# Neighborhood attention on one core: values projected for two strips at once, emptied over all 128 partitions, with a transfer of one half

## The chip, the core and the metric

One core of a Trainium2 chip runs the kernel. The metric is the device time in microseconds (us) of one execution; a time quoted for a kernel is the median of its runs, each beside runs of the kernel before on the same chip.

In the profile PE is the matmul engine, PEld its weight load, DVE the vector engine, ACT the scalar engine, POOL the engine called GpSimd, and SP the engine that only issues transfers here.

## The reference, cut to what matters

```python
x: [1, 224, 224, 192] bf16      wqkv: [192, 576]      wo: [192, 192]
ks, dil = 7, 2                                  # a 7 x 7 neighborhood, every second row and column
q, k, v = split(x @ wqkv)
...                                             # indices of the 49 neighbors of each pixel, clipped at the edges
logits = einsum('bnc,bnkc->bnk', q, k[neighbors]) * 192 ** -0.5
p = softmax(logits)
out = einsum('bnk,bnkc->bnc', p, v[neighbors]) @ wo
```

## The kernel before

The picture has 14 strips of 16 rows. Dilation 2 splits rows and columns into even and odd: `rc` is the row parity and `cc` the column parity. A **step** (rc, j) makes 8 rows of one parity around the border between strips j-1 and j. There are 28 steps, in the order (0,0), (1,1), (0,1), (1,2), (0,2), (1,3) and so on. A step has 7 **ticks**. In each tick PE makes 16 score matmuls (`s_stage`), ACT takes exp of them, PE makes 8 value matmuls into the one `y` bank (`v_stage`), and DVE takes reciprocal and product out of that bank (`out_stage`). The remaining slot of a tick goes to a **filler**: value projections for the next step (`v_unit`), or one of four query and edge items.

The weights are folded, so the "keys" are x itself, only rearranged. A strip is read by one transposing load into `xt`; POOL then copies it, parity by parity, into `XA` and `XB`; and both the scores and the value projections read those copies.

```python
def load_xt(b):                                  # one strip, 4 buffers, all on SP's queue
    t = xt_pool.tile([128, 3, 16, S], BF, name=f"xt{b}", tag="xt")
    nc.sync.dma_start_transpose(out=..., in_=xp[16 * (b % NJ): ...])

def make_keys(k, rc):                            # four copies on POOL
    for cc in range(2):
        for kt in range(2):
            key_copy(k, rc, cc, kt, nc.gpsimd.tensor_copy)

def half(k, cc):
    return 64 * ((k + cc) % 2)                   # which 64 partitions strip k has in VW

def v_unit(k, rc, n0, n1):                       # one strip, 4 tiles of columns: 16 matmuls
    def emit():
        pv = ps_go.tile([128, 2, 2, 256], F32, name="pv", tag="go")
        for n in range(n0, n1):
            for kt in range(2):
                for cc in range(2):
                    h = half(k, cc)
                    nc.tensor.matmul(pv[h:h + 64, ..., 0:C], lhsT=keys(k, rc, cc, kt)[:, n, :],
                                     rhs=WP[:, cc, kt, :], start=(kt == 0), stop=(kt == 1))
        for cc, eng in ((0, nc.vector.tensor_copy), (1, nc.scalar.copy)):
            hs = slice(half(k, cc), half(k, cc) + 64)
            eng(out=VW[hs, rc, cc, n0:n1, 0:C], in_=pv[hs]...)        # 64 partitions x 768
        ...                                       # the two are declared independent
    return emit

# the loop over the steps, cut to the parts in question
    if rc == 1 or si == 0:
        load_xt(j + 2)                           # at the start of step (1, j)
    for ti, i in enumerate(range(NQ - 1, -1, -1)):
        T = s_stage(rc, j, i)
        if pend:
            v_stage(pend)
            out_stage(pend)
        ...                                      # fillers: projections, query items
        if ti == 2 and si + 2 < len(steps) and si > 0:
            make_keys(steps[si + 2][1], steps[si + 2][0])
```

The softmax here doesn't subtract the row's maximum and nothing guards it: scores larger than these inputs give would overflow.

## Time and profile before

The time before was 352.73 us (median of 3 runs, 351.33 to 355.38).

| what | busy us | share of the span |
|---|---|---|
| PE | 317.1 | 90% |
| DVE | 261.8 | 74% |
| ACT | 254.1 | 72% |
| POOL | 248.6 | 71% |

The page of the kernel before: busy times, the TensorE clock over 40 slices of the span (9 is 90% or more), the transfers, the chain of work that ended last by engine, and the groups (busy us, mean ns of one, then idle time just before it and what ended most of that).

```profile
PE 317.1 (90%) x7686; PEld 290.5 (83%) x7686; DVE 261.8 (74%) x554; ACT 254.1 (72%) x414; POOL 248.6 (71%) x525
...
PEclk9998999999999999999999999999999999999995
...
DMA packets 112369, 43.81 MB, mean 125 GB/s; under 512 B 86900, under 2 KB 111838, under 8 KB 112290
...
PE 56%; DVE 29%; issue 7%; POOL 2%; ACT 2%; DMA 1%; POOLq 0%; DVEq 0%
...
L482 DVE TENSOR_TENSOR o_sb<-y,rs 128x384 bf16<-128x384 f32 x162 | 101.1, 624 | 6.2 <-DVE rs L477 0.6
L286 ACT CAST vw<-pv 64x768 bf16<-64x768 f32 (+2 forms) x116 | 82.7, 713 | 31.5 <-PE pv L281 21.0
L286 DVE CAST vw<-pv 64x768 bf16<-64x768 f32 (+2 forms) x116 | 98.7, 851 | 2.2 <-PE pv L281 0.3
```

Two readings matter. First, PE is busy nine tenths of the time and is most of the chain; DVE is the next in it. Second, the evictions of the projections (`vw<-pv`) cost DVE 98.7 us and ACT 82.7 us, and each uses only 64 of the 128 partitions.

PE's waits in the kernel before (us in total, times, longest):

```profile
PE y L432 <- DVE o_sb L482: 11.9, 52, 0.9
PE y L432 <- ACT p_sb L419: 2.9, 2, 2.6
```

And the timeline of DVE in the middle of the run (start, length), which shows where the first of them comes from:

```profile
168.31 0.56 DVE L482 TENSOR_TENSOR o_sb<-y,rs 128x384 bf16<-128x384 f32 x1
168.90 0.96 DVE L286 CAST vw<-pv 64x768 bf16<-64x768 f32 x1
169.90 0.17 DVE L477 RECIPROCAL rs<-y 128x2 f32<-128x2 f32 x1
170.10 0.56 DVE L482 TENSOR_TENSOR o_sb<-y,rs 128x384 bf16<-128x384 f32 x1
```

DVE works in order. An eviction of 0.96 us sits between two turns of the `y` bank, and the value matmuls of the next tick can't start before the product at 170.10 has ended.

### The profile page before, as it was taken

How to read it: one execution, taken by the hardware profiler on the slowest of the kernel's cores; microseconds unless marked ns; L12 is line 12 of the kernel's file. 1: busy time of each engine (PE TensorE's matmuls, PEld its weight loads, DVE VectorE, ACT ScalarE, POOL GpSimd, SP SyncE). 2: the span in 40 equal slices, each digit the busy share in tenths (PEclk: the TensorE clock that was granted, in tenths of full speed). 3: DMA queues.
4: the chain of work that ended last, by engine and by line, in shares of the span. 5: the costliest groups of instructions: out<-in, count | busy, mean ns of one | idle time of the engine just before them, and what ended most of it. 6: DMA issues, size and time to landing. Idle time of an engine off the chain costs nothing.

```text
span 351.5 us, 17929 instructions
## 1 busy us (share of the span) xinstructions
PE 317.1 (90%) x7686; PEld 290.5 (83%) x7686; DVE 261.8 (74%) x554; ACT 254.1 (72%) x414; POOL 248.6 (71%) x525
## 2 busy tenths in 40 slices
PE   8969899999999899998999999999899999999850
PEld 5549789988899789998889998899888999988740
DVE  8687897777777687786787777877677787768750
ACT  3437888877788688787877878778777688768730
POOL 7497988676786669666776678666785678757670
PEclk9998999999999999999999999999999999999995
DMA  8975583864928728365293472834928539222112
GB/s 190 198 172 137 131 193 105 149 157 93 185 80 123 161 62 202 83 152 133 63 188 98 103 185 60 195 91 98 188 72 135 150 73 208 72 67 68 40 43 81
DMA packets 112369, 43.81 MB, mean 125 GB/s; under 512 B 86900, under 2 KB 111838, under 8 KB 112290
## 3 DMA queue, kind: packets, MB, share of 16 engines
q1 hardware_dynamic: 109490, 41.06, 52.3%
q0 software_dynamic: 2432, 1.39, 1.6%
q8 instruction: 60, 0.98, 1.2%
q10 hardware_dynamic: 368, 0.22, 0.2%
q14 instruction: 19, 0.16, 0.2%
HBM read 0.29 MB, written 19.35 MB: 56 GB/s over the span
## 4 chain that ended last, share of the span: by engine, by line
PE 56%; DVE 29%; issue 7%; POOL 2%; ACT 2%; DMA 1%; POOLq 0%; DVEq 0%
PE y L432 19%; DVE o_sb L482 15%; PE pg L357 12%; PE pv L281 8%; DVE vw L286 7%; PE s_88 L416 5%; DVE rs L477 5%; PE pe L313 4%; PE s_87 L416 4%; PE y L185 1%; POOL out_dram L449 1%; DVE oall L482 1%; DMA out_dram<-o_sb 1%; ACT vw L286 1%; DVE xa_90 L256 1%
## 5 line engine op out<-in xcount | busy, mean ns | idle before, releaser
L432 PE MATMUL y<-vw,p_sb 128*48 128x193 bf16 (+1 forms) x1540 | 104.3, 249 | 19.0 <-DVE o_sb L482 11.9
L482 DVE TENSOR_TENSOR o_sb<-y,rs 128x384 bf16<-128x384 f32 x162 | 101.1, 624 | 6.2 <-DVE rs L477 0.6
L286 ACT CAST vw<-pv 64x768 bf16<-64x768 f32 (+2 forms) x116 | 82.7, 713 | 31.5 <-PE pv L281 21.0
L286 DVE CAST vw<-pv 64x768 bf16<-64x768 f32 (+2 forms) x116 | 98.7, 851 | 2.2 <-PE pv L281 0.3
L432 PEld LDWEIGHTS <-p_sb 128*48 128x48 bf16 (+1 forms) x1540 | 75.9, 106 | 28.6 <-issue 22.5
L477 DVE RECIPROCAL rs<-y 128x2 f32<-128x2 f32 x168 | 28.5, 170 | 63.0 <-PE y L432 61.7
L419 ACT ACTIVATE p_sb<-s_88 128x448 bf16<-128x448 f32 x98 | 53.5, 546 | 14.2 <-PE s_88 L416 13.7
L447 POOL DMA_DIRECT2D out_dram<-o_sb x27 | 15.6, 577 | 63.8 <-DVE o_sb L482 63.8
L419 ACT ACTIVATE p_sb<-s_87 128x448 bf16<-128x448 f32 x98 | 53.4, 545 | 4.3 <-PE s_87 L416 3.6
L357 PEld LDWEIGHTS <-aw 128*64 128x64 bf16 x1008 | 52.1, 112 | 4.4 <-DVE vw L286 1.4
L416 PEld LDWEIGHTS <-xa_91 128*64 128x64 bf16 x532 | 50.6, 111 | 1.1
L416 PEld LDWEIGHTS <-xa_90 128*64 128x64 bf16 x532 | 49.4, 111 | 2.4 <-DVE ga_98 L361 1.1
L416 PEld LDWEIGHTS <-xa_92 128*64 128x64 bf16 x476 | 45.5, 111 | 1.2
L416 PEld LDWEIGHTS <-xb_94 128*64 128x64 bf16 x420 | 38.3, 111 | 2.0 <-issue 1.3
L416 PEld LDWEIGHTS <-xb_93 128*64 128x64 bf16 x420 | 36.3, 111 | 0.9
L361 ACT CAST hs<-pg 128x848 bf16<-128x848 f32 x27 | 23.4, 865 | 16.4 <-PE pg L357 7.9
L416 PEld LDWEIGHTS <-xb_95 128*64 128x64 bf16 x364 | 32.2, 111 | 1.0
L416 PEld LDWEIGHTS <-xb_96 128*64 128x64 bf16 x336 | 30.2, 111 | 0.6
L281 PE MATMUL pv<-WP,xa_90 128*64 128x192 bf16 x280 | 28.2, 248 | 0.3 <-DVE vw L286 0.3
L281 PE MATMUL pv<-WP,xa_91 128*64 128x192 bf16 x280 | 27.7, 246 | 0.2 <-DVE vw L286 0.2
L361 ACT CAST ga_98<-pg 128x848 bf16<-128x848 f32 x27 | 23.4, 865 | 5.1 <-PE pg L357 4.0
L361 ACT CAST ga_99<-pg 128x848 bf16<-128x848 f32 x26 | 22.5, 865 | 4.2 <-PE pg L357 3.0
(231 smaller groups left out, 1038.2 us busy)
## 6 DMA issues: line engine op xcount, KB each, us to landing
out_dram<-o_sb SPq DMA_DIRECT2D x162, 96.0 KB
out_dram<-o_sb SPq DMA_DIRECT2D x27, 60.0 KB
out_dram<-oe POOLq DMA_DIRECT2D x27, 18.0 KB, 3.1
out_dram<-o_sb POOLq DMA_DIRECT2D x27, 18.0 KB, 2.7
xb_95<-xb_93 SPq DMA_DIRECT2D x4, 112.0 KB
xb_96<-xb_94 SPq DMA_DIRECT2D x4, 112.0 KB
out_dram<-oall SPq DMA_DIRECT2D x8, 36.0 KB
out_dram<-oall POOLq DMA_DIRECT2D x8, 36.0 KB, 2.1
```

The lines of the kernel that those rows point to most:

```text
L185: nc.tensor.matmul(y_bank[:, 1, 1, 0:128], lhsT=ident[:], rhs=ident[:], start=True, stop=True, skip_group_check=True)
L281: nc.tensor.matmul(pv[h:h + 64, (n - n0) // 2, (n - n0) % 2, 0:C], lhsT=keys(k, rc, cc, kt)[:, n, :], rhs=WP[:, cc, kt, :], start=(kt == 0 ...
L286: ins.append(eng(out=VW[hs, rc, cc, n0:n1, 0:C], in_=pv[hs].rearrange("p a b c -> p (a b) c")[:, 0:n1 - n0, 0:C]))
L313: nc.tensor.matmul(pg[64 * h:64 * h + 64, g, par::2, :], lhsT=AW[w][:, 64 * h:64 * h + 64], rhs=r, start=(i == 0), stop=(i == 1))
L357: nc.tensor.matmul(pr[64 * h:64 * h + 64, g, a_ - 4 * g:b_ - 4 * g, :], lhsT=AW[w][:, 64 * h:64 * h + 64], rhs=xt[b][:, k, l, :], start=(i ...
L361: return eng(out=dst[:, 6:S].rearrange("p s (g r) -> p s g r", r=4), in_=pr[ps, :, :, 3:S - 3].rearrange("p g r s -> p s g r"))
L416: nc.tensor.matmul(o[h:h + 64, :, rs], lhsT=keys(k, rc, cc, kt)[:, n, :], rhs=(A, Bt)[kt][:, cc, CW * n:CW * n + QW, rs], start=(kt == 0), ...
L419: nc.scalar.activation(out=T.p[:].rearrange("p a b -> p (a b)"), in_=ps[:, 0:4 * QW * BR], func=ACTF.Exp)
L432: nc.tensor.matmul(o, lhsT=l, rhs=rhs, start=st, stop=True, skip_group_check=True)
L447: q.dma_start(out=dst, in_=src[8 * s0:8 * s1])
L477: nc.vector.reciprocal(out=rs[:], in_=y_bank[:, sls, :, C:C + 1])
L482: nc.vector.tensor_tensor(out=o[:], in0=y_bank[:, sls, :, 0:C], in1=rs[:].to_broadcast([128, nt, 2, C]), op=ALU.mult)
```

## The change: its intent, and the diff

The intent is to make each eviction shorter. The columns of one strip fill 64 partitions of the bank, those of the next strip the other 64. If two strips, k and k+1, are projected together, an eviction of 128x384 carries as many elements as one of 64x768, with half as many per partition. But the pairs are (0, 1), (2, 3) and so on, and a step (rc, j) needs strips j-1 and j: where j is even these belong to different pairs, so one half has to move into the neighboring block, by an SBUF-to-SBUF transfer. The change also pairs the edge items (24 matmuls of 96 columns for two strips in place of 48 of 48), lets query items stream 424 columns in place of 448, and reorders the start and the end. It also narrows the score matmuls at the two ends of a row and moves the query item of tick 1 ahead of the value matmuls.

The core of the diff (cuts marked):

```diff
-    xt_pool = ctx.enter_context(tc.tile_pool(name="xt", bufs=4))
+    XT = const.tile([128, 4, 3, 16, S], BF, name="xt")        # strip b in slot (b + 3) % 4
-    VW = const.tile([128, 2, 2, NT, VS], BF, name="vw")
+    VW = [const.tile([128, 2, 2, NT, VS], BF, name=f"vw{k}") for k in range(2)]
...
+    def move_half(rc, k, dst, src, n0, n1):
+        for cc in range(2):
+            h = slice(half(k, cc), half(k, cc) + 64)
+            nc.sync.dma_start(out=VW[dst][h, rc, cc, n0:n1].rearrange("p n c -> p (n c)"),
+                              in_=VW[src][h, rc, cc, n0:n1].rearrange("p n c -> p (n c)"))
...
+    def v_pair(k, rc, n0):                                     # two strips, 2 tiles of columns: 16 matmuls
+        def emit():
+            pv = ps_go.tile([128, 2, 2, 256], F32, name="pw", tag="go")
+            for n in (n0, n0 + 1):
+                for cc in range(2):
+                    for kt in range(2):
+                        for s in (k, k + 1):
+                            h = half(s, cc)
+                            nc.tensor.matmul(pv[h:h + 64, n - n0, cc, 0:C], lhsT=keys(s, rc, cc, kt)[:, n, :],
+                                             rhs=WP[:, cc, kt, :], start=(kt == 0), stop=(kt == 1))
+            for n, eng in ((n0, nc.scalar.copy), (n0 + 1, nc.vector.tensor_copy)):
+                eng(out=VW[k // 2 % 2][:, rc, :, n, 0:C], in_=pv[:, n - n0, :, 0:C])
+        return emit
...
     def edge_item(b):
+        nb = 2 if b else 1                                     # strips b and b + 1 together
...
-                                             rhs=xt[b][:, k, l, :], start=(i == 0), stop=(i == 1))
+                                             rhs=xt[b][:, k, l, 3:S - 3], start=(i == 0), stop=(i == 1))
...
+    value_weights()                                            # after the first query items
     v0 = v_units(0, 0)
     v0.pop(0)()
+    load_xt(2)                                                 # was after onehot_rows(1)
     spread_onehots(0)
...
+    def values_of(si):                                         # which pair in which tick
...
+        if rc == 1 and j % 2 == 1:
+            return list(zip((2, 4, 5, 6), v_pairs(j + 1, 1)[:4]))
...
+    def moves_of(si):
...
+        if rc == 1 and j % 2 == 0:
+            a = (0, j, (j - 2) // 2 % 2, j // 2 % 2)
+            return [(3, a + (8, NT)), (6, a + (0, 8))]
...
-        if rc == 1 or si == 0:
-            load_xt(j + 2)
...
+            while m_q and m_q[0][0] == ti:
+                move_half(*m_q.pop(0)[1])
...
+            if rc == 0 and j % 2 == 1 and ti == 1 or rc == 1 and j % 2 == 0 and ti == NQ - 1:
+                if j + 3 <= NJ:
+                    load_xt(j + 3)
...
+                if rc == 0 and j % 2 == 0 and ti == 5 and j + 3 < NJ:
+                    make_keys(j + 3, 1)
```

The built program adds one thing that the source doesn't say. Before, the two evictions of a filler were declared independent; in `v_pair` they are not, and each DVE half waits for the ACT half of its pair.

## The prediction

> **What bounds the kernel now.** PE is busy 90% of the span (the page), about 95% in the steady state (table of windows: 21.1 of 22 us), at clock 1.00. Not all of that streams. In the PE timeline from 164 to 187 us a tick is 16 score matmuls (0.36 us), 8 value matmuls (0.33) and one filler: 16 projections (0.66) or a query item (0.75). Unblocked, the scores' slot is 0.34 to 0.40 us; in about half of the ticks it is 0.69 to 0.73. There PE waits for y: DVE must take reciprocal (0.17) and product (0.56) out of the y bank before the next value matmuls. The DVE timeline shows why it is late: it has just begun a 64x768 eviction of vw (0.95 us) when the value matmuls end (vw from 168.90, reciprocal only at 169.90, PE at 170.71). So steady state is PE plus a y loop through DVE; the chain of waits agrees (PE 56%, DVE 29%). The slots' excess is 2.8 us per two steps of 22.5, some 35 us in all.
>
> **What the change does.**
> - vw evictions, 116 on DVE (98.7 us) and 116 on ACT (82.7), become about 100 each, mostly of 128x384; at 0.55 and 0.47 us (the groups' times for this width) DVE loses some 40 us, ACT 30. PE's projections stay.
> - But the built program's order shows that each DVE half now waits for the ACT half of its pair (before, both waited for PE alone). DVE works in order, so much of what an eviction saves can come back.
> - Fillers are spread unevenly: one of four steps has no projections, so three ticks are bare. The last steps of before show a bare tick: 1.39 us, the y loop alone, against 0.69 of PE work.
> - Query items stream 424 columns instead of 448: 3 us in all. Edge items: half as many, twice as wide. Now 24 matmuls of 48 columns take 1.07 us, 45 ns each, while scores of 84 to 112 columns take 22. The Trainium skill (SBUF — State Buffer, Door 1: The DMA port swizzle) says that accesses leaving a 16-byte line pay a penalty, which fits the old read, 224 bytes per element; the new one has runs of three. I expect about 1 us per new item: 5 to 7 us less PE work.
> - New: about 0.7 MB of SBUF-to-SBUF moves per two steps. DMA is half busy, though each transpose fills it for 5 to 6 us. Moves have 4 or more ticks until their use: no PE wait expected.
> - Start: value weights after the first queries, two key copies later: 2 us. End: a third store queue, perhaps 1.5 of the last 10 us.
>
> **Sum.** A recurrence of my own over these durations (engines in order, y bank, two filler buffers), an estimate, gives 45.7 us per four steps for before (measured 45.0) and 44.6 for after; without the ACT-to-DVE wait 43.1. That is 6 us over the steps, 15 without that wait. With start and end: 341 us, 330 to 350. Faster by over 2%: 0.74, same 0.23, slower 0.03.
>
> **What would show it.** DVE busy down by 35 to 45 us, ACT by 25 to 35, PE by about 8; PE's waits on o_sb still there, now in the bare ticks and behind late evictions; DVE idle before vw ended by ACT; no wait on moves; steps of 10 us (bare) and 11.5.
>
> **What would make it wrong.** The pair wait may be hidden (330). Moves stuck behind a transpose would hold the value matmuls (slower). Edge items may cost 2 us. Start-up may gain more.

## The result, and the profile after

The changed kernel took **375.62 us** (median of 4 runs, 374.66 to 376.81) against 353.42 (4 runs) of the kernel before. The ratio is 1.063, with a 95% interval of 1.056 to 1.070: it is slower. A ratio is the mean time of one kernel's fast runs over that of the other's of the same rounds, so it is not quite the ratio of the quoted medians. Executions over 1.5% slower than the fastest of the same kernel are left out of the means.

The page of the changed kernel, the same parts:

```profile
PE 315.5 (85%) x7493; PEld 284.3 (76%) x7493; DVE 219.2 (59%) x532; ACT 225.0 (60%) x409; POOL 239.6 (64%) x509
...
PEclk9998996999999999899998999989999899999988
...
DMA packets 116472, 53.40 MB, mean 143 GB/s; under 512 B 87784, under 2 KB 112610, under 8 KB 116394
...
PE 48%; POOL 17%; DMA 14%; issue 9%; DVE 8%; ACT 1%; SPq 1%; ACTq 1%; POOLq 0%; DVEq 0%
PE y L468 13%; PE pw L289 12%; PE pg L392 10%; DMA xt<-in_x_dram 10%; PE s_83 L452 4%; PE s_84 L452 4%; DVE o_sb L520 3%; PE y L193 2%; POOL out_dram L483 2%; POOL xb_93 L266 1%; POOL xb_91 L266 1%; POOL gb_99 L409 1%; DMA vw_95<-vw_94 1%; 
...
L292 DVE CAST vw_94<-pw 128x384 bf16<-128x384 f32 x49 | 27.3, 557 | 26.1 <-ACT vw_94 L292 26.0
```

The engines did what they were meant to: DVE lost 42.6 us of busy time and ACT 29.1. But the chain has changed its character. DVE fell from 29% to 8% of it, and POOL (17%) and DMA (14%) have come in; the loads of x alone (`DMA xt<-in_x_dram`) are 10% of the span. Before, POOL and DMA were 3% together.

PE's waits in the changed kernel:

```profile
PE y L468 <- DVE o_sb L520: 10.4, 26, 0.9
PE y L468 <- ACT p_sb L455: 5.7, 7, 3.8
...
PE pw L289 <- DMA xb_91<-xb_91: 4.2, 1, 4.2
PE pw L289 <- POOL xb_93 L266: 3.7, 6, 0.7
PE pw L289 <- POOL xb_91 L266: 2.6, 4, 0.7
...
PE pw L289 <- POOL xa_89 L266: 2.2, 4, 0.7
...
PE pw L289 <- POOL xa_87 L266: 1.6, 3, 0.5
...
PE y L468 <- DMA vw_94<-vw_95: 0.5, 1, 0.5
...
PE y L468 <- DMA vw_95<-vw_94: 0.2, 1, 0.2
```

The projections of a pair (`pw`) wait for key copies, a wait that did not exist before. (The `xb_91<-xb_91` of 4.2 us is a single wait in the start, for rows of constants that SP spreads over the key buffers; e4_spread_first takes it up.) The last two lines are the waits for the moved halves: 0.7 us in all.

**Where the time went, by steps.** Once per step DVE begins the reciprocal of the last columns (`rse`), so its start is a clock on each step. I took the 28 readings from DVE's timeline (us):

```
                            before    after   difference
to the 1st reading           25.5     24.7      -0.7
1st to 4th (3 steps)         39.1     52.1     +13.0
4th to 24th (20 steps)      225.3    236.9     +11.7
24th to 28th (4 steps)       44.4     41.8      -2.6

from the 4th reading on, before: 11.2 11.3 11.3 10.6 12.3 11.4 11.3 10.6 12.2 11.3 11.3 10.6 ...
from the 4th reading on, after:  11.6  9.9 13.0 11.1 11.2 10.2 15.1 11.1 11.2 10.6 14.9 11.1 ...
```

So there are two places: the first three steps, and every fourth step later, which takes about 15 us (15.1, 14.9, 14.8, 14.3; the first of them only 13.0). Most other steps after are as fast as or slightly faster than before (three took 11.6 to 12.4). The 10 us steps are those without projections, as predicted.

**One long step.** In the long steps, (1, j) with odd j, the first pair of the next two strips is projected. The chain of waits of the changed kernel from 130 to 152 us (start, length, what), at the seventh of the steps listed:

```profile
133.86 9.95 DMA xt<-in_x_dram
...
144.81 0.93 POOL xb_93 L266
145.74 0.88 POOL xa_89 L266
...
146.68 0.94 POOL xb_93 L266
...
147.66 0.56 PE pw L289 x9
```

The load takes 9.95 us from its issue to its landing; then come four key copies of 0.93 us each, one after the other; and the projection comes with the last. SP's timeline shows what stands just ahead of the load in its queue:

```profile
132.57 1.19 SPq L258 DMA_DIRECT2D vw_95<-vw_94  x2
133.86 7.64 SPq L71 DMA_TRANSPOSE xt<-in_x_dram  x1
```

It is the second of the step's two moves, one transfer for each column parity. For some 5 us after 133.86 the transfer records show the moves, stores and then little else; the load's own stretch of 290 GB/s runs only from about 139 to 143.3, so it ends about 9.5 us after the issue. SP's timeline of the kernel before has a load, too:

```profile
130.49 6.17 SPq L70 DMA_TRANSPOSE xt_3722<-in_x_dram  x1
```

Its stretch of 290 GB/s began at about 133.5 and ended at about 138.3, 7.8 us after its issue. The Trainium skill (DMA: Bandwidth & Descriptors, section Queues, rings and completion order) says that SP's transfers have one ring on each of the 16 DMA engines, consumed in ring order; this trace agrees in so far as the load's stretch starts only when the moves and stores are through. Not all of a long transit comes from moves, though: see e2_no_moves and e12_own_queue.

PE's timeline shows how the pair's 16 matmuls (0.66 us where nothing is missing) are let through one copy at a time (in brackets: idle time before, and what ended it):

```profile
145.79 0.27 PE L289 MATMUL pw<-WP,xb_93 128*64 128x192 bf16 x1 [0.60 <-POOL xb_93 L266]
...
146.67 0.27 PE L289 MATMUL pw<-WP,xa_89 128*64 128x192 bf16 x1 [0.52 <-POOL xa_89 L266]
...
147.66 0.27 PE L289 MATMUL pw<-WP,xb_93 128*64 128x192 bf16 x1 [0.72 <-POOL xb_93 L266]
```

The slot of this pair is 3.25 us, from 144.77 to 148.02: 2.6 too long. PE then runs at half clock, as the table of windows shows (stretch, its length, busy us and instruction count of PE, PEld, DVE, ACT and POOL, then the granted clock, the DMA share, GB/s):

```profile
145.00:147.00 2.00, 0.81 (x7) 0.27 (x6) 0.73 (x2) 0.00 (x0) 1.94 (x3) 1.00 0.56 148
147.00:149.00 2.00, 1.34 (x32) 1.34 (x34) 0.19 (x1) 0.55 (x2) 1.83 (x6) 0.81 0.53 139
149.00:151.00 2.00, 2.00 (x28) 1.92 (x25) 1.10 (x3) 0.54 (x2) 1.82 (x7) 0.50 0.19 49
151.00:153.00 2.00, 2.00 (x56) 2.00 (x54) 0.73 (x2) 1.57 (x3) 1.96 (x3) 0.84 0.27 65
```

From 149 to 151 the granted clock is 0.50, and the query item there takes 1.42 us in place of 0.73. The Trainium skill (TensorE: Matmul & The Clock Gate, Part 1: The HAM clock gate) states that the matmul array falls to half its clock when it has been idle for a window of about 3.4 us, and needs about as long to come back. The trace agrees on the half clock (0.50 and nothing lower in these windows) and on its length: windows of 0.81, 0.50 and 0.84 come to about 3.4 us at half clock, an estimate from the table. It does not agree on the trigger, since PE was never idle that long here (see the last section). A long step is 3.7 us longer than a step with nothing missing (mean of 15.1, 14.9, 14.8 and 14.3, minus 11.1): 2.6 of that is the pair's wait in the step shown, and about 1.1 is left for the clock. The step of 13.0 us fits this: its first pair waited for the last two key copies as well (0.5 and 0.7 us), but its clock stayed at 1.00.

**The cause as a theory.** A pair (k, k+1) needs the keys of strip k+1, so it needs each second strip earlier than a single unit would. The load of that strip can't be issued much earlier, because its buffer still holds a strip that the query item of tick 5 reads; it goes out in tick 6, behind the moves. The rival theories were that the moves themselves hold the value matmuls; that the wait of DVE for ACT within a pair eats the gain; that the reordered start is at fault by itself; and that shorter evictions would have gained nothing anyway.

### The profile page after: what moved, and what is told of

Same layout as the page of the kernel before. It is cut to its first block, busy times and chain, and to the rows that moved or that the text cites. A ratio compares the mean times of both kernels' runs of the same rounds, so it can differ in the third digit from the quotient of the medians.

```text
span 372.9 us, 17630 instructions
## 1 busy us (share of the span) xinstructions
PE 315.5 (85%) x7493; PEld 284.3 (76%) x7493; DVE 219.2 (59%) x532; ACT 225.0 (60%) x409; POOL 239.6 (64%) x509
## 4 chain that ended last, share of the span: by engine, by line
PE 48%; POOL 17%; DMA 14%; issue 9%; DVE 8%; ACT 1%; SPq 1%; ACTq 1%; POOLq 0%; DVEq 0%
PE y L468 13%; PE pw L289 12%; PE pg L392 10%; DMA xt<-in_x_dram 10%; PE s_83 L452 4%; PE s_84 L452 4%; DVE o_sb L520 3%; PE y L193 2%; POOL out_dram L483 2%; POOL xb_93 L266 1%; POOL xb_91 L266 1%; POOL gb_99 L409 1%; DMA vw_95<-vw_94 1%; DVE rs L515 1%; DVE oe L507 1%
## 5 line engine op out<-in xcount | busy, mean ns | idle before, releaser
L468 PEld LDWEIGHTS <-p_sb 128*64 128x64 bf16 (+1 forms) x1540 | 78.3, 108 | 38.2 <-issue 21.7
L392 PE MATMUL pg<-xt,aw 128*64 128x106 bf16 (+3 forms) x1008 | 83.2, 297 | 0.5 <-DVE vw_95 L292 0.3
L468 PE MATMUL y<-vw_94,p_sb 128*64 128x193 bf16 (+1 forms) x770 | 54.0, 255 | 16.3 <-DVE o_sb L520 6.3
L468 PE MATMUL y<-vw_95,p_sb 128*64 128x193 bf16 (+1 forms) x770 | 53.5, 252 | 9.9 <-DVE o_sb L520 4.1
L292 DVE CAST vw_94<-pw 128x384 bf16<-128x384 f32 x49 | 27.3, 557 | 26.1 <-ACT vw_94 L292 26.0
L452 PEld LDWEIGHTS <-xa_86 128*64 128x64 bf16 x420 | 39.9, 115 | 3.2 <-issue 2.5
L289 PE MATMUL pw<-WP,xb_91 128*64 128x192 bf16 x196 | 36.2, 250 | 6.8 <-DMA xb_91<-xb_91 4.2
L452 PEld LDWEIGHTS <-xa_87 128*64 128x64 bf16 x420 | 39.9, 114 | 1.6 <-issue 1.2
L292 ACT CAST vw_94<-pw 128x384 bf16<-128x384 f32 x49 | 23.5, 479 | 27.5 <-PE pw L289 24.0
L452 PEld LDWEIGHTS <-xb_91 128*64 128x64 bf16 x420 | 37.4, 114 | 2.4 <-issue 2.0
L289 PE MATMUL pw<-WP,xa_86 128*64 128x192 bf16 x196 | 38.0, 248 | 1.0 <-ACT vw_95 L314 1.0
L452 PEld LDWEIGHTS <-xb_90 128*64 128x64 bf16 x420 | 37.9, 115 | 0.7
L289 PE MATMUL pw<-WP,xb_90 128*64 128x192 bf16 x196 | 38.2, 249 | 0.0
L289 PE MATMUL pw<-WP,xa_87 128*64 128x192 bf16 x196 | 36.8, 249 | 1.6 <-POOL xa_87 L266 1.6
L292 DVE CAST vw_95<-pw 128x384 bf16<-128x384 f32 x42 | 23.4, 556 | 21.9 <-ACT vw_95 L292 21.9
L292 ACT CAST vw_95<-pw 128x384 bf16<-128x384 f32 x42 | 20.1, 479 | 25.4 <-PE pw L289 25.1
```

The costliest lines, as they stand in the source:

```text
L289: nc.tensor.matmul(pv[h:h + 64, n - n0, cc, 0:C], lhsT=keys(s, rc, cc, kt)[:, n, :], rhs=WP[:, cc, kt, :], start=(kt == 0), stop=(kt == 1))
L292: eng(out=VW[k // 2 % 2][:, rc, :, n, 0:C], in_=pv[:, n - n0, :, 0:C])
L392: nc.tensor.matmul(pr[64 * h:64 * h + 64, g, a_ - 4 * g:b_ - 4 * g, :], lhsT=AW[w][:, 64 * h:64 * h + 64], rhs=xt[b][:, k, l, 3:S - 3], st ...
L452: nc.tensor.matmul(o[h:h + 64, s0:s1, rs], lhsT=keys(k, rc, cc, kt)[:, n, :], rhs=(A, Bt)[kt][:, cc, CW * n + s0:CW * n + s1, rs], start=( ...
L468: nc.tensor.matmul(o, lhsT=l, rhs=rhs, start=st, stop=True, skip_group_check=True)
```

## The experiments

Medians are beside the median of the kernel before of the same call (353.13, 352.33, 351.8 and 352.76 us). "4th" is the absolute time of the 4th reading, "middle" the 20 steps from the 4th to the 24th. I use the absolute 4th reading to compare starts, because the prologue up to the first reading took either about 25 or about 29 us in kernels with the same start: in one profile the granted clock between 12 and 16 us was 1.00 (after), in another 0.50 (e3_no_pair_wait). The clock does not settle it: in e4_spread_first and e5_start_dve it was 1.00 there, and their first readings still came at 29 us.

| run | median us | ratio (95% interval) | 4th | middle |
|---|---|---|---|---|
| before | | | 64.6 | 225.3 |
| after | 375.62 | 1.063 (1.056 to 1.070) | 76.9 | 236.9 |
| e1_same_keys (result wrong) | 361.53 | 1.025 (1.019 to 1.031) | 77.6 | 222.7 |
| e2_no_moves (result wrong) | 361.60 | 1.025 (1.021 to 1.029) | 76.5 | 224.8 |
| e3_no_pair_wait | 376.48 | 1.067 (1.063 to 1.071) | 76.1 | 239.9 |
| e4_spread_first | 378.93 | 1.071 (1.065 to 1.077) | 78.9 | 240.6 |
| e5_start_dve | 376.59 | 1.068 (1.060 to 1.075) | 78.3 | 238.2 |
| e6_load_sooner | 368.96 | 1.047 (1.040 to 1.053) | 76.0 | 231.0 |
| e7_all | 370.75 | 1.050 (1.043 to 1.056) | 77.3 | 233.6 |
| e8_edges_only | 352.36 | 0.998 (0.993 to 1.004) | 66.8 | 222.7 |
| e9_edges_later | 351.91 | 1.000 (0.995 to 1.004) | 67.3 | 221.3 |
| e10_ceiling (result wrong) | 348.00 | 0.988 (0.983 to 0.992) | 69.3 | 216.8 |
| e11_half_evict (result wrong) | 346.41 | 0.984 (0.979 to 0.989) | 67.2 | 217.3 |
| e12_own_queue | 392.18 | 1.110 (1.102 to 1.117) | (slow run) | (slow run) |
| e13_third_load | 349.18 | 0.993 (0.989 to 0.997) | 65.1 | 221.3 |
| e14_even_fillers (result wrong) | 337.52 | 0.958 (0.955 to 0.961) | 64.9 | 212.2 |

### The first call: take away one suspect each

**e1_same_keys** takes away the need for the second strip's keys; the result is wrong.

```diff
-   nc.tensor.matmul(pv[h:h + 64, n - n0, cc, 0:C], lhsT=keys(s, rc, cc, kt)[:, n, :],
+   nc.tensor.matmul(pv[h:h + 64, n - n0, cc, 0:C], lhsT=keys(k, rc, cc, kt)[:, n, :],
```

> Wrong result on purpose: each paired projection takes the keys of its first strip for both halves, so that the matmuls, evictions and moves stay as they are, but nothing waits for the second strip's keys. Theory (the pairs need the second strip's keys one strip earlier than before, and load plus key copies come too late): the steps of about 15 us go back to about 11.3, four times 3.5 us, and most of the 13 us lost in the first three steps goes too; 350 to 354 us instead of 375. Rival (the moves load DMA, or the evictions hold each other up): no change, over 370 us.

It took 361.53 us. The middle fell by 14.2 us to 222.7, below that of the kernel before, and the long steps were gone (11.1 to 11.2 where they took about 15; the longest step of the middle, of another kind, took 13.3). So the second strip's keys are what the long steps wait for. The start did not get shorter at all, though, and that is why the time missed what I expected. Its waits show new ones in the place of the old:

```profile
PE y L468 <- DVE o_sb L520: 13.5, 25, 3.9
PE y L468 <- DMA vw<-vw: 8.6, 6, 4.9
```

Relieved of the keys, PE runs into the moves (`vw<-vw`, up to 4.9 us in one wait).

**e2_no_moves** leaves the moves out from the third step on; the result is wrong.

```diff
-                move_half(*m_q.pop(0)[1])
+                m = m_q.pop(0)[1]
+                if si < 2:
+                    move_half(*m)
```

> Wrong result on purpose: the transfers of half a block are left out but for the first one. Rival (transfers compete with the loads and hold PE): all of the loss goes, about 353 us. Theory (late keys): the transfers matter only as far as they stand ahead of the load in its queue; the load would land 2 to 4 us sooner, the long steps shrink from 15 to about 12, the first three steps stay as long as they are (52 us from the first to the fourth end reading); 362 to 367 us.

It took 361.60 us, and the middle fell by 12.1 us to 224.8: the long steps went from about 15 to 11.8 (one to 12.6). In the kernel after PE waited for moves for no more than 0.7 us in all, yet taking them away is worth 12 us. They cost through the load that queues behind them, and mostly through its issue: counted back from the reading of the long step, SP issued the load 9.9 to 10.3 us ahead in the kernel after and 12.0 to 12.3 us ahead here (in e6_load_sooner, below, 13.8 to 15.3, and its long steps took 11.1). From its issue the load itself was not reliably shorter without moves: 7.5 to 9.4 us to the end of its stretch in three steps, and 11.2 to its landing in a fourth, where the four loads of the kernel after took 9.4 to 10.0 to their landing. The two experiments remove the same long steps from two ends, so their gains don't add up: both keys and moves are needed to make the stall.

**e3_no_pair_wait** declares the two evictions of a pair independent, as the single units had it; the result is right.

```diff
+            ins = []
             for n, eng in ((n0, nc.scalar.copy), (n0 + 1, nc.vector.tensor_copy)):
-                eng(out=VW[k // 2 % 2][:, rc, :, n, 0:C], in_=pv[:, n - n0, :, 0:C])
+                ins.append(eng(out=VW[k // 2 % 2][:, rc, :, n, 0:C], in_=pv[:, n - n0, :, 0:C]))
+            tc.declare_no_dep(ins[1].ins, ins[0].ins, reason="...")
```

> Right result: the wait of each DVE half of an eviction on the ACT half of its pair is declared needless, as in the kernel before. Rival (serial evictions cause the loss): about 353 us. Theory (late keys): the waits for keys stay, four steps of 14 to 15 us are still there, and only the steps without a stall shorten by 0.3 to 0.4 us each, so 366 to 371 us.

It took 376.48 us, no gain: a miss. In steps with nothing missing it saved 0.2 us of 11.1, but a faster step only arrives at the same missing keys earlier. The wait of DVE for ACT, which the prediction feared most, is not what makes the kernel slow.

**e4_spread_first** puts the third load of the start back behind the spreading of the one-hot rows (the constants that mask what is no neighbor); the result is right.

```diff
     v0.pop(0)()
-    load_xt(2)
     spread_onehots(0)
...
     spread_onehots(1)
+    load_xt(2)
     make_keys(1, 1)
```

> Right result: the third load is issued after the spreading of the one-hot rows, as in the kernel before, instead of ahead of it. If the first paired projection waits because those spreads queue behind the third load (4.2 us in the trace), the first step shortens by 4 to 5 us and the total is about 370 to 371 us; if Pool's key copies bind there anyway, no change, 374 to 376 us. The later steps must not change.

It took 378.93 us, also a miss. The wait of 4.2 us for `xb_91<-xb_91` is gone, but POOL's key copies of the start ran 1.1 us later, waits of 2.5 us for moves came in, and the 4th reading came 2 us later, not sooner. This profile also had the late first reading (29.1 us), so not all of the 2 us need be the edit's.

### The second call: mend the start and the order, and the small parts alone

**e5_start_dve** makes three of the sets of key copies of the start on DVE, which is busy for 59% of the span only; the result is right.

```diff
-                make_keys(2, 1)
+                make_keys(2, 1, nc.vector.tensor_copy)
             if si == 1 and ti == 2:
-                make_keys(3, 1)
-                make_keys(2, 0)
+                make_keys(3, 1, nc.vector.tensor_copy)
+                make_keys(2, 0, nc.vector.tensor_copy)
```

> Right result: the twelve key copies for strips 2 (both row parities) and 3 (the first parity) go to DVE, which is about 60% busy, instead of Pool. Theory for the first three steps (Pool is busy without a gap from 33 to 72 us with key copies that the pairs want a strip earlier, so Pool binds): from the first to the fourth end reading 43 to 46 us instead of 52, the total 367 to 370. Rival (the queue of loads and one-hot spreads binds): 52 us and 375 as before. The later steps stay as in the changed kernel.

It took 376.59 us, a miss. A copy that takes POOL 0.93 us takes DVE 0.39 to 0.45 here, but eight of them in a burst stand before the products in DVE's order: PE's longest wait for `o_sb` rose from 0.9 to 3.7 us. One stall was changed for another.

**e6_load_sooner** issues the load one tick sooner, right after the last reader of its buffer, and puts the last part of the move behind it; the result is right.

```diff
-            return [(3, a + (8, NT)), (6, a + (0, 8))]
+            return [(4, a + (4, NT)), (6, a + (0, 4))]
...
-   if rc == 0 and j % 2 == 1 and ti == 1 or rc == 1 and j % 2 == 0 and ti == NQ - 1:
+   if rc == 0 and j % 2 == 1 and ti == 1 or rc == 1 and j % 2 == 0 and ti == NQ - 2:
```

> Right result: in the even steps of odd rows the next load is issued at the sixth tick, right after the last query item that reads its buffer, and the half transfer that stood ahead of it is split so that only 4 of 14 tiles go after the load. Theory (late load of the second strip, made later by the transfers ahead of it in the queue): load lands 3 to 4 us sooner, the four steps of 15 us become 11.3 to 12.3, 360 to 364 us; the first three steps stay at 52. Rival (loads are slow because transfers run at the same time, whatever the order): long steps stay above 14, 374 or more.

It took 368.96 us: faster than the kernel after by about 6 us, but less than expected. The long steps are gone (all took 11.1; the longest step of the middle, its first, took 13.0). All moves are still made, and a load still took about 9.5 us (131.63 to 141.1), but it was issued 13.8 to 15.3 us ahead of the step's reading; so what counts is when the load goes out, and not the mere presence of the moves. PE's waits say what came in their place:

```profile
PE y L468 <- DMA vw<-vw: 7.9, 8, 1.9
...
PE pw L289 <- POOL xb L266: 1.2, 2, 0.6
...
PE pw L289 <- POOL xa L266: 1.2, 2, 0.7
```

The waits for keys have nearly gone, and 7.9 us of waits for moves have come: now a part of the moves stands behind the load. With the load and the moves in one queue, one of them is late. (e12_own_queue shows that two queues do not mend it.)

**e7_all** has the edits of e3, e4, e5 and e6 together; the result is right.

> Right result: key copies of the start on DVE, the third load after the spreads, the load sooner, no wait within a pair. If the losses are the two that the theory names and nothing else, the steady steps sum to 43.5 to 44.5 us per four (before 45.0) and the start costs no more than before: 345 to 351 us, faster than the kernel before by 0.5 to 2%. If a third cost remains, over 356 us.

It took 370.75 us, a clear miss of what I expected. Its waits for moves were 14.0 us in 12 times, and for `o_sb` 16.7 us in 31. The single mends don't add up; the waits suggest that each of them hands its time to the next owner of the same queue or engine, but no run shows this by itself.

**e8_edges_only** is the kernel before with only the paired edge items and the shorter query items; the result is right. The core of its edit is `edge_item` as in the diff of the change, with `XT` in one tile.

> Right result: the kernel before with the narrower query items and the paired edge items alone (no paired values, no transfers). My sum for these two was 5 to 7 us of PE work at 1 us per new edge item; the trace after shows 0.71 us for one, so 3 us from the queries and about 8 us from the edges. Where PE waits for the y bank anyway part of it is lost: 345 to 350 us, faster than before by 1 to 2%. If PE work is hidden behind the y loop: 352 to 354.

It took 352.36 us, no difference, a miss. The middle gained 2.6 us, and the 4th reading came 2.3 later. My reading is that a paired item for strips 1 and 2 needs strip 2 before a single one would, the same mistake in small. The profile does not show it: the one wait of the paired item there, 1.8 us, ends with an eviction of ACT. The PE work did fall, from 317.1 to 309.2 us.

### The third call: the ceiling, and where the limits are

**e9_edges_later** pairs only from strip 2 on; the result is right.

```diff
-        t = XT[:, (b + 3) % 4]
+        t = XT[:, (b + 2) % 4]
...
-        nb = 2 if b else 1
+        nb = 2 if b >= 2 and b < NJ else 1
```

> Right result: as e8_edges_only, but strips 0 and 1 keep an edge item each and pairs begin with strips 2 and 3, so that step 0 waits for no third strip. In e8 the steady steps gained (22 us less 19.4 for eight steps by the end readings: 222.7 us from the fourth to the 24th against 225.3), and the start lost 2.3 us. Expected: start as before or 0.5 us less, 348 to 350 us, 1% faster than before. If the start of e8 had another cause: 351 to 353.

It took 351.91 us: the middle was 221.3, but the start was no better, because the pair of strips 2 and 3 now waited for strip 3:

```profile
PE pe L318 <- DMA xt<-in_x_dram: 2.7, 1, 2.7
```

**e10_ceiling** joins e1, e2 and e3: pairs without the second strip's keys, without moves and without the pair's own wait. The result is wrong; it tells what the change could be worth at most if all its inputs came in time.

> Wrong result on purpose: paired values with the first strip's keys for both, no transfers, no wait within a pair, that is the change with all of its suspected costs taken away in the steady steps. What is left is what paired evictions and the new order of fillers are worth. From the fourth to the 24th end reading, before has 225.3 us. My recurrence gives 214 us (222.9 with the pair wait; the run with the first strip's keys measured 222.7). If evictions are not what bounds the steady steps, 222 or more. The start is still long (45 to 52 us for three steps), total 348 to 358.

It took 348.00 us, ratio 0.988. The middle is 216.8 us, 8.5 below that of the kernel before. The 4th reading came at 69.3 us, where it was 76.9 after, 77.6 in e1_same_keys and 76.5 in e2_no_moves: with one cause gone nothing comes back in the start, with both gone 7 to 8 us do. So the start seems to suffer from the same two causes, tightly packed, so that the removal of one only exposes the other. (e10_ceiling has e3's edit too, which alone moved the 4th reading by 0.8 us; e1 and e2 were not run together without it.) The 4.7 us that remain to the 64.6 of the kernel before lie ahead of the first step: this profile had one of the slow prologues, with its first reading at 29.5 us in place of 25.5, and its next three steps took 39.7 us, against 39.1 before.

**e11_half_evict** is the kernel before with evictions of half the columns; the result is wrong. It asks what shorter evictions alone are worth.

```diff
-                ins.append(eng(out=VW[hs, rc, cc, n0:n1, 0:C],
-                               in_=pv[hs]...[:, 0:n1 - n0, 0:C]))
+                ins.append(eng(out=VW[hs, rc, cc, n0:n1, 0:C // 2],
+                               in_=pv[hs]...[:, 0:n1 - n0, 0:C // 2]))
```

> Wrong result on purpose: the kernel before, with each eviction of values copying half of its columns (64x384 instead of 64x768 on DVE and ACT), all else the same. It tests the premise of the change and of the prediction, that the evictions on DVE hold up the y bank. If so, the recurrence gives 212 us instead of 228.7 from the fourth to the 24th end reading, that is 16 us less: about 209 measured, total 335 to 339. If PE's own work bounds: no change, 350 or more.

It took 346.41 us, and the middle fell by 8.0 us, half of the 16 that my recurrence gave for it. PE's waits for `o_sb` fell from 11.9 us in 52 times to this:

```profile
PE y L432 <- DVE o_sb L482: 6.5, 19, 0.9
```

So shorter evictions do help, and there the intent of the change was right; but they are worth about 2%.

**e12_own_queue** moves the transfers of the halves to ACT's queue. It has the edits of e3 and e4 too, the load one tick sooner, one of the moves a tick later, and eight of the key copies of the start spread over ticks of DVE; the result is right.

```diff
-            nc.sync.dma_start(out=VW[dst][h, rc, cc, n0:n1]...
+            nc.scalar.dma_start(out=VW[dst][h, rc, cc, n0:n1]...
```

> Right result: the changed kernel with the half transfers on the ACT queue, the second of the even ones a tick later, the load right after its last reader, the third load after the spreads, key copies of the start spread over ticks on DVE, no wait within a pair. If queueing of transfers and loads behind each other, and bursts of key copies, are the costs, the steps of 14 to 15 us are gone (11 to 11.8), the first three sum to 44 to 48, total 350 to 358. If the shared DMA engines are the limit and not the queue, waits on transfers or keys of 5 us and more stay, total above 362.

It took 392.18 us, the slowest of all; its three fast runs took 388.4 to 393.0, ratio 1.110. The profiled run was its slow one (397.2 us), so I take from it only what the waits and timelines name:

```profile
PE y L470 <- ACT p_sb L457: 22.8, 17, 7.1
PE y L470 <- DMA vw<-vw: 17.8, 10, 3.7
```

The 7.1 us came once, in the start: ACT issued two moves at 43.4 and 47.9 us, and the exps behind them began at 48.5. The profile ends that wait with another transfer (`gb<-gb`), so what the moves waited for is not settled. Later waits for exps were at most 2.0 us, but for one of 3.8 at the end that the kernel after has too. Nor did the moves come sooner: one issued at 140.5 landed 11.4 us later, and the load issued at 136.9, with no move in its queue, took about 15. The Trainium skill (DMA: Bandwidth & Descriptors, section Issuing engines are not separate DMA queues) says that transfers started by different engines run on the same 16 DMA engines and interleave, and that only the issue time is saved; the 17.8 us of waits for moves here agree. So the outcome is the one that I expected if the shared DMA engines and not the queue were the limit; since this run changed several things at once, it shows that a second queue did not help, and no more.

### The fourth call: what is left open, and a version that beats both

Two things were open: whether the small parts can be had without the loss in the start, and why e10_ceiling gains only 8.5 us in the middle although it has both shorter evictions and less PE work (e8's gain of 2.6 is in it). The suspect was the uneven spread of the fillers: ticks without one.

**e13_third_load** is e9_edges_later with strip 3 loaded in the first step; the result is right.

```diff
             if si == 0 and ti == 0:
+                load_xt(3)
                 mask_rows(3, 2, nc.gpsimd.tensor_copy)
```

> Right result: as e9_edges_later, with the load of strip 3 issued in step 0 instead of step 1 (its buffer is free from the start). In e9 the edge item of strips 2 and 3 waited 2.7 us for this load and PE's clock fell to half after it; the first three steps took 42.2 us against 39.1 before. If that is the whole loss: 38.5 to 39.5 us for three steps, steady 221 as in e9, total 347.5 to 349.5, faster than before by 0.7 to 1.2%. If pairing has another cost at the start: 351 to 353.

It took **349.18 us** (6 runs, 348.64 to 351.94), ratio 0.993 with an interval of 0.989 to 0.997. The first three steps took 39.6 us (39.1 before), and the middle kept its 221.3. It is faster than both kernels, if by less than 1%, which is clear of the noise; two slow runs of the kernel before (357.4 and 357.3) are not counted.

**e14_even_fillers** adds the half evictions of e11 to e13, with the fillers of the kernel before, evenly spread; the result is wrong.

> Wrong result on purpose: e13 with evictions of half the columns, so query and edge items of the change, half the eviction time, no transfers and no pairing of values, and the even order of fillers of before. From the fourth to the 24th end reading e10 (same savings, but one step of four without projections) had 216.8 us. If the bare ticks of the uneven order cost what I wrote (three per four steps, 0.7 us each, 10 us in all) this one has 205 to 210; if the uneven order costs nothing, 215 to 218. Total 330 to 338 or 341 to 346.

It took 337.52 us, ratio 0.958; its middle was 212.2. That is 4.6 us below e10_ceiling, which has evictions of the same length and, but for strip 1, the same edge and query items, but three bare ticks in one of four steps. In the middle PE is busy 200.7 us in e10_ceiling and 201.9 here, so its work is the same, but its waits for DVE's products (`o_sb` and `oe`) are 11.7 us there and 3.3 here. So the uneven fillers are the likely owner of the 4.6 us, between the two numbers that I had written; the two kernels also differ in the order of the key copies and in the score matmuls, which no run takes apart. What a bare tick costs shows in DVE's timeline of the kernel before, in its last step:

```profile
335.43 0.17 DVE L477 RECIPROCAL rs<-y 128x2 f32<-128x2 f32 x1 [0.62 <-PE y L432]
335.64 0.56 DVE L482 TENSOR_TENSOR o_sb<-y,rs 128x384 bf16<-128x384 f32 x1
336.82 0.17 DVE L477 RECIPROCAL rs<-y 128x2 f32<-128x2 f32 x1 [0.62 <-PE y L432]
```

Without a filler the tick still takes 1.39 us (335.43 to 336.82), since the next value matmuls wait for the product; PE has only 0.7 us of work in it.

## Why the prediction was wrong, point by point

**The step that failed** stands in two sentences of it: "PE's projections stay." and "Moves have 4 or more ticks until their use: no PE wait expected." The first counted the pair's matmuls and took their inputs as given. The second asked when the *result* of a move is needed, and there it was nearly right (0.7 us of waits), but not what the move delays. The runs showed in their place a chain that the sum did not have: the moves stand before the load of each second strip in SP's queue, which then goes out some 2 us later than without them (e2_no_moves); the load lands 9.95 us after its issue; four key copies of 0.93 us follow on POOL; and the first pair waits for the last of them, 2.6 us, with about 1.1 us at half clock afterwards. The four long steps with 3.7 us more each make 14.7 us (15.1 + 14.9 + 14.8 + 14.3 - 4 x 11.1); taking the keys' need away gave 14.2 (e1_same_keys), taking the moves away gave 12.1 (e2_no_moves). My recurrence had engines, banks and buffers in it, but neither POOL's copies nor the queue of the loads, although the change moved every second load from the start of a step to its end. The prediction named a stuck move as its danger; it was the load that got stuck behind the move.

**The start** was put at 2 us more and came out at 12.3 (4th reading, 76.9 less 64.6). The same two causes seem to do most of it: with both gone (and the pair's own wait, e10_ceiling) the 4th reading comes 7.6 us sooner, with one gone no more than 0.3 sooner. Mending its single waits (e4, e5) was worth nothing.

**The wait of DVE for ACT** was put at 9 us over all steps. It is there (26.0 us of DVE's idle time before `vw_94` and 21.9 before `vw_95` end with ACT), but it is mostly hidden: e3_no_pair_wait saves 0.2 us in a step with nothing missing, some 4 to 5 us if all of the steps were such, and none in fact.

**The busy times** came as predicted: DVE -42.6 (35 to 45 predicted), ACT -29.1 (25 to 35). PE fell by only 1.6 us where 8 were predicted. e10_ceiling has the same 7493 matmuls and 305.3 us, 10.2 less than the kernel after, so what is missing is not more work; at half clock, where a query item takes 1.42 us in place of 0.73, the same work counts as longer busy time; e8_edges_only has the same two items and shows -7.9.

**The edge items** were a little better than the estimate of about 1 us: 24 matmuls of 96 columns take 0.71 us, 30 ns each, where 24 of 48 columns took 1.07, 45 ns each. That agrees with what the prediction drew from the Trainium skill (SBUF — State Buffer, Door 1: The DMA port swizzle) on accesses that leave a 16-byte line; no run here separates that from other differences of the two forms.

**The gain of the steps without stalls** was nearly right for the kernel after: 44.6 us per four steps predicted, 44.5 measured in e1_same_keys (222.7 over 5). But the recurrence had 45.7 for the kernel before, which has 45.1; so even with its inputs in time the gain would have been half of what I wrote. It was built on an excess of 35 us in PE's slots that the evictions seemed to own; in fact halving the evictions gives back 8 us of the middle (e11_half_evict), and with the new edge and query items 13 (e14_even_fillers, 225.3 to 212.2).

**The end** gained 2.6 us in the last four steps (from the 24th reading to the 28th), and nothing after them. No run separates the third queue from the bare steps there.

Two things stay open. The first is what sets the prologue at 25 or 29 us; the clock differs in some of the profiles, but not in e4_spread_first and e5_start_dve, and no run here controls it. The second is whether pairs could work with a fifth buffer for strips, so that the load could be issued a step earlier; that was not tried.

## What to carry to other kernels

Before work on two inputs is joined, ask for the second input: when is its load issued, what frees its buffer, what stands before it in its queue, and how long is it from landing to usable? A transfer put into the queue of the loads is not free merely because its own result has time; it costs what it delays. And the time that a change frees on an engine beside the critical path is worth only what the loop through the shared bank returns, here 8.5 of some 72 us (42.6 on DVE and 29.1 on ACT), with some 2.6 of the 8.5 from PE's lighter items (e8_edges_only); so measure that ceiling first, with a kernel that is allowed to be wrong.

## What the Trainium skill lacked or had wrong

- TensorE: Matmul & The Clock Gate, Part 1: The HAM clock gate, names an idle window of about 3.4 us as what halves the clock, and under another heading short idle times between groups of matmuls. Here PE was not idle so long: between 145 and 149 us it was busy 0.81 and then 1.34 of 2 us, its three waits were 0.60, 0.52 and 0.72 us, and the granted clock still fell to 0.50 (149 to 151 us). Waits with single matmuls in between were enough here; the page doesn't say what share of activity keeps the clock up.
- DMA: Bandwidth & Descriptors, section Latency and other measured facts, gives a transposing load 261 GB/s with a non-contiguous middle dimension and some 350 to 400 in the contiguous case. The records here show about 290 GB/s while a load runs alone, but the load's stretch ended 7.8 us after its issue in the kernel before and 9.5 us behind moves; the page has no figure for that time.
- DMA: Bandwidth & Descriptors, section Issuing engines are not separate DMA queues, names the saved issue time as the one use of a second issuing engine. The page also says that a transfer's wait for a semaphore is taken on the issuing engine, but it gives no figure for what that costs an engine with other work: on ACT, two moves held the exps for 7.1 us once (e12_own_queue).
- No page that I read gives the time of a rearranging copy on POOL beside DVE: 128x896 in bf16 took 0.93 us on POOL and 0.39 on DVE (e5_start_dve; four such copies in the start of the kernel before took DVE 0.71 each).
